# First batch of a spectral mixing and SwiGLU kernel: the first two chunks by turns, weights rounded in halves and loaded from ScalarE's queue

## The chip, the cores and the metric

One core of one Trainium2 chip. The metric is the device time in microseconds (us) of one execution. Each timed run is compared with runs of the kernel before on the same chip, in the same job.

## The reference

```python
X = np.fft.rfft(x, axis=1)                    # x: 8 x 3008 x 256
y = np.fft.irfft(X * (filt_r + 1j * filt_i)[None], n=3008, axis=1)
t = y.reshape(24064, 256)
g = t @ w_gate                                # 256 x 1536
out = (g / (1 + np.exp(-g)) * (t @ w_val)) @ w_out
```

## The kernel before

Each batch passes through a Fourier transform in two stages with tables, a filter, the inverse transform (stage 3 ends it) and the feed-forward part. That part works on four chunks of tokens; a chunk takes six blocks (`hidden`, one for each sixth of the 1536 columns) and, after every third of them, a projection (`project`). The products use a seven-product scheme for 2x2 blocks, so each of the 18 pieces of weight needs seven planes of 128 x 128 in memory: four from the weight, three sums. The next batch's transform fills in between.

The weights come as float64. They are turned to float32 by hand ("rounding"): VectorE takes mantissa and exponent apart, ScalarE converts, VectorE puts together, GpSimd multiplies both parts and makes the sums. This is done in the first 228 us, while the first batch runs. The parts that matter:

```python
def load_weights(j, queue=nc.sync):
    if j < len(weights):
        raws[j] = rpool.tile([128, 2, 2, 128, 2], U32, name=f"raw_{j}", tag="raw", bufs=2)
        for i in range(2):
            ins = queue.dma_start(out=raws[j][:, i], in_=weights[j][0][:, i])
            ...
def round_weights(j, following=True):
    if following:
        load_weights(j + 2)
    raw, (_, dst, left) = raws.pop(j), weights[j]
    low, high = raw[:, :, :, :, 0], raw[:, :, :, :, 1]
    pw = rpool.tile([128, 2, 2, 128], U32, name=f"pw_{j}", tag="pw")     # one buffer
    w = rpool.tile([128, 2, 2, 128], FP32, name=f"w_{j}", tag="w")       # one buffer
    ...  # VectorE: w <- high, pw <- high; ScalarE: w, pw; VectorE: pw, pw <- raw, w <- raw
    pin(e.tensor_tensor(out=dst[:, 0:4, :]..., in0=w, in1=pw.bitcast(FP32), op=ALU.mult))
    ...  # GpSimd: the four sums
for i in range(NP):                    # the blocks of a batch
    k, j = divmod(i, NJ)
    ...
    for _ in range((2, 3, 2, 2, 2, 3)[i] if todo else 0):
        round_weights(todo.pop(0))
    hidden(b, k, j, cur.y[k], fill)
```

A scheduler settles each engine's order when the kernel is built.

Of the kernel before, what the change touches and what calls it, by code (L numbers as in the profile page):

```python
# [34 lines left out]
FP32 = mybir.dt.float32  # L35
U32 = mybir.dt.uint32
AF = mybir.ActivationFunctionType
ALU = mybir.AluOpType
# [6 lines left out]
NJ = NM // 2  # L45
# [8 lines left out]
NCHUNK = 32 // NW  # L54
TH = NH * NR
TOK = (0, 128, TH - 128)
NQB = 2
JB = NJ // NQB
# [45 lines left out]
def kernel(  # L104
# [10 lines left out]
    nc = tc.nc  # L115
# [5 lines left out]
    def pool(name, bufs, space=None):  # L121
        kw = {} if space is None else {"space": space}
        return ctx.enter_context(tc.tile_pool(name=name, bufs=bufs, **kw))
# [19 lines left out]
    wv_t = cpool.tile([128, NJ, 7, 128], FP32)  # L143
# [17 lines left out]
    def add(eng, dst, a, b):  # L161
        eng.tensor_tensor(out=dst, in0=a, in1=b, op=ALU.add)  # L162

    def sub(eng, dst, a, b):
        eng.tensor_tensor(out=dst, in0=a, in1=b, op=ALU.subtract)  # L165
# [3 lines left out]
    def weight_parts():  # L169

        cols = [w.bitcast(U32).rearrange("(a p) (h j f two) -> j p h a f two",
                                         a=2, p=128, h=2, j=NJ, two=2)
                for w in (moe_w_gate, moe_w_val)]
        rows = moe_w_out.bitcast(U32).rearrange("(l j p) (c f two) -> j p l c f two",
                                                l=2, j=NJ, p=128, c=2, two=2)
        def hid(j):
            for w, dst in zip(cols, (wg_t, wv_t)):
                yield w[j], dst[:, j], True

        for q in range(NQB):  # L180
            for j in range(JB * q, JB * q + JB):
                yield from hid(j)
            for j in range(JB * q, JB * q + JB):
                yield rows[j], wo_t[:, j], False

    weights = list(weight_parts())
    raws = {}

    def load_weights(j, queue=nc.sync):
        if j < len(weights):  # L190
            raws[j] = rpool.tile([128, 2, 2, 128, 2], U32, name=f"raw_{j}", tag="raw", bufs=2)
            for i in range(2):
                ins = queue.dma_start(out=raws[j][:, i], in_=weights[j][0][:, i])
                if j in (2, 3):
                    tc.keep_in_program_order(ins)

    def round_weights(j, following=True):



        if following:
            load_weights(j + 2)
        raw, (_, dst, left) = raws.pop(j), weights[j]
        low, high = raw[:, :, :, :, 0], raw[:, :, :, :, 1]
        pw = rpool.tile([128, 2, 2, 128], U32, name=f"pw_{j}", tag="pw")
        w = rpool.tile([128, 2, 2, 128], FP32, name=f"w_{j}", tag="w")
        man = w.bitcast(U32)
        v = nc.vector
        flat = "p a b f -> p (a b f)"
        flat2 = "p a b f two -> p (a b f) two"  # L210

        pin = tc.keep_in_program_order
        pin(v.tensor_scalar(out=man, in0=high, scalar1=0xFFFFF, scalar2=None,
                            op0=ALU.bitwise_and))
        pin(nc.scalar.activation(out=w, in_=man, func=AF.Copy, scale=2.0 ** -20, bias=1.0))
        pin(v.tensor_scalar(out=pw, in0=high, scalar1=20, scalar2=0x7FF,
                            op0=ALU.logical_shift_right, op1=ALU.bitwise_and))
        pin(nc.scalar.activation(out=pw, in_=pw, func=AF.Relu, bias=off_t))
        v.tensor_scalar(out=pw, in0=pw, scalar1=255.0, scalar2=2.0 ** 23,
                        op0=ALU.min, op1=ALU.mult)  # L220
        v.scalar_tensor_tensor(out=pw.rearrange(flat), in0=raw.rearrange(flat2)[:, :, 1],
                               scalar=0x80000000, in1=pw.rearrange(flat),
                               op0=ALU.bitwise_and, op1=ALU.bitwise_or)
        v.scalar_tensor_tensor(out=w.rearrange(flat), in0=raw.rearrange(flat2)[:, :, 0],
                               scalar=2.0 ** -52, in1=w.rearrange(flat),
                               op0=ALU.mult, op1=ALU.add)

        e = nc.gpsimd
        pin(e.tensor_tensor(out=dst[:, 0:4, :].rearrange("p (a b) f -> p a b f", b=2), in0=w,  # L229
                            in1=pw.bitcast(FP32), op=ALU.mult))  # L230
        if left:
            a11, a12, a21, a22, s1, s2, s4 = [dst[:, i] for i in range(7)]
            add(e, s1, a21, a22)
            sub(e, s2, s1, a11)
            sub(e, a21, a11, a21)
            sub(e, s4, a12, s2)
        else:
            b11, b12, b21, b22, t1, t2, t4 = [dst[:, i] for i in range(7)]
            sub(e, t1, b12, b11)
            sub(e, t2, b22, t1)  # L240
            sub(e, b12, b22, b12)
            sub(e, t4, b21, t2)
# [3 lines left out]
    def bank(kind, name):  # L246
        return wps.tile([128, 512], FP32, name=f"w{kind}_{name}", tag=kind)

    def warm(count, width=4):


        for i in range(count):
            ps = bank("F", "idle")[:, 0:128 * width]
            tc.keep_in_program_order(nc.tensor.matmul(
                out=ps, lhsT=wv_t[:, 0, 0, :],
                rhs=wv_t[:, 0, 0:width, :].rearrange("p i f -> p (i f)"), start=True, stop=True))

    class Spectral:

# [277 lines left out]
    rpool = pool("raw", 1)  # L537
    todo = list(range(len(weights)))
# [7 lines left out]
    with tc.tile_pool(name="start", bufs=1) as spool0:  # L546
        for i in range(4):
            spec.load_x(i)
        spec.load_tables()
        load_weights(0, nc.scalar)  # L550
        load_weights(1, nc.scalar)
        nc.sync.dma_start(out=wi_t, in_=wi_dram.ap())
        nc.vector.memset(wv_t[:, 0], 0.0)
        warm(5)
        for u in range(N_ONE):
            spec.stage1(u)
            warm(1, 2)
        warm(6)
        for _ in range(2):
            round_weights(todo.pop(0), False)  # L560
        lag = 3
        for u in range(N_TWO + lag):
            if u < N_TWO:
                spec.stage2a(u)
            if u >= lag:
                spec.stage2b(u - lag)
    for j in (2, 3):
        load_weights(j)
    for i in range(2):
        spec.load_t4(0, i)  # L570
    warm(9)
# [2 lines left out]
    for _ in range(2):  # L574
        round_weights(todo.pop(0))
# [1 line left out]
    spool = pool("sp", 2)  # L577
    hpool = pool("hp", JB + 1)
    upool = pool("up", 2)
    opool = pool("op", 1)  # L580



# [2 lines left out]
    for b in range(B):  # L586
        cur = spec
        work = {}

        def at(i, piece):  # L590
            work.setdefault(i, []).append(piece)

        for k in range(1, NCHUNK):
            for i in range(2):
                at(NJ * (k - 1) + 1 + i, lambda k=k, i=i: cur.load_t4(k, i))
            for step in range(4):
                at(NJ * (k - 1) + 3 + step // 2, lambda k=k, step=step: cur.stage3(k, step))
        if b + 1 < B:
            spec = Spectral(b + 1)
            nxt = spec  # L600
            for u in range(N_ONE):
                at(u // 2, lambda u=u: nxt.stage1(u))
            for u in range(N_TWO + 1):
                if u:
                    at(9 + u, lambda u=u: nxt.stage2b(u - 1))
                if u < N_TWO:
                    at(9 + u, lambda u=u: nxt.stage2a(u))
            for i in range(2):
                at(22, lambda i=i: nxt.load_t4(0, i))
            for step in range(4):  # L610
                at(NP - 1, lambda step=step: nxt.stage3(0, step))

        for i in range(NP):
            k, j = divmod(i, NJ)
            pieces = work.get(i, [])
            first = (len(pieces) + 1) // 2
            fills = [pieces[:first], pieces[first:]]

            def fill(fills=fills):
                for piece in fills.pop(0):  # L620
                    piece()

            for _ in range((2, 3, 2, 2, 2, 3)[i] if todo else 0):
                round_weights(todo.pop(0))
            hidden(b, k, j, cur.y[k], fill)
            if late is not None:
                project(*late)
                late = None
            if j % JB == JB - 1:
                late = (b, k, j // JB)  # L630
# [31 lines left out]
```

## Time and profile before

| | before |
|---|---|
| time, median of 3 runs | 3118.65 us (3118.13 to 3119.42) |
| TensorE busy over the span | 98% |
| first product of stage 3 on TensorE | 103.0 us |
| last rounding instruction of VectorE starts | 222.5 us (ends 223.2) |

TensorE is the bound from 246 us on. All that can be won lies before. The prediction shows the lines.

To follow this I keep one ledger for every kernel. From the trace of TensorE I count its products up to a moment, one by one, give each the start-to-start distance that it has where TensorE is full (0.3157 us for 376 columns, 0.1117 for 128, 0.11 for 94, 0.43 for 512, 0.2155 for 256; warm-up products count nothing), and subtract the sum from the elapsed time. The rest is **lost time**. It needs no wait list, and sees slow clocks as well as gaps (in the kernel before, with a granted clock of 0.51 from 164 to 168 us, pairs of products of 376 columns took 1.34 to 1.62 us, later 0.80). Some records can be missing from a trace, so 1 or 2 us in it mean nothing.

### The profile page before, as it was taken

The numbers are of one execution on the slowest core, as the hardware profiler recorded it, in microseconds if no ns is written. First come the engines' busy times: TensorE is split into PE (matmuls) and PEld (weight loads), VectorE is DVE, ScalarE is ACT, GpSimd is POOL, SyncE is SP. The second block draws the span as 40 slices with busy tenths as digits, with TensorE's granted clock in tenths as the row PEclk, the third lists the DMA queues.
The fourth block names the chain that finished last, engine by engine and source line by source line (L and its number), as shares of the span: only waits on it lengthen the run. The fifth ranks groups of instructions, "written<-read, shape, count | busy, mean of one in ns | idle before, by whom it ended". The sixth has DMA issues, their size and how long they took to land.

```text
span 3116.7 us, 41163 instructions
## 1 busy us (share of the span) xinstructions
PE 3056.4 (98%) x15560; PEld 2240.5 (72%) x15560; DVE 1476.5 (47%) x2348; ACT 1140.3 (37%) x2070; POOL 1405.8 (45%) x1622
## 2 busy tenths in 40 slices
PE   7789999999999999999999999999999999999999
PEld 4457777777767777767777777767777677777776
DVE  4664553354543554345543455434553444544443
ACT  0443333333343343343333333343333433333333
POOL 3574454444543444444543454434544344533343
PEclk8999999999999999999999999999999999999999
DMA  8432222222212222222222132121322222200000
GB/s 233 130 117 68 72 81 56 61 76 68 75 55 72 59 79 60 61 68 81 69 60 65 57 88 71 51 71 55 91 68 56 63 63 68 68 28 21 21 6 16
DMA packets 123634, 212.51 MB, mean 68 GB/s; under 512 B 23670, under 2 KB 69750, under 8 KB 122578
## 3 DMA queue, kind: packets, MB, share of 16 engines
q1 hardware_dynamic: 91692, 132.25, 14.8%
q0 software_dynamic: 24448, 68.71, 7.7%
q10 hardware_dynamic: 7296, 8.92, 1.1%
q8 instruction: 123, 2.02, 0.3%
q14 instruction: 75, 0.61, 0.1%
HBM read 134.81 MB, written 74.97 MB: 67 GB/s over the span
## 4 chain that ended last, share of the span: by engine, by line
PE 80%; POOL 7%; DVE 6%; issue 3%; DMA 2%; ACT 2%; SPq 0%; POOLq 0%; ACTq 0%; DVEq 0%
PE wA_v L435 15%; PE wA_g L435 15%; PE wA_o L499 7%; PE wE_v L435 7%; PE wE_g L435 7%; PE wE_o L499 7%; PE wF_o L499 4%; PE wF_g L435 4%; PE pd L396 3%; PE wF_v L435 3%; POOL o L162 3%; PE pa L332 3%; POOL h L165 3%; PE pc L376 2%; PE pb L356 2%
## 5 line engine op out<-in xcount | busy, mean ns | idle before, releaser
L435 PE MATMUL wA_v<-y,wv_t 128*128 128x376 f32 x1536 | 612.5, 480 | 7.3 <-ACT u_v L444 4.3
L435 PE MATMUL wA_g<-y,wg_t 128*128 128x376 f32 x1536 | 614.3, 481 | 4.4 <-POOL wg_t L229 3.5
L165 POOL TENSOR_TENSOR h<-h 128x376 f32<-128x376 f32 x576 | 566.9, 984 | 28.8
L162 POOL TENSOR_TENSOR h<-h 128x376 f32<-128x376 f32 x192 | 188.4, 981 | 701.2 <-PE wE_v L435 389.1
L444 ACT COPY u_g<-wA_g 128x376 f32<-128x376 f32 x576 | 269.5, 468 | 589.9 <-PE wA_g L435 587.6
L435 PEld LDWEIGHTS wA_v<-y,wv_t 128*128 128x128 f32 x1536 | 289.2, 190 | 204.0 <-DVE h L457 15.6
L499 PEld LDWEIGHTS wA_o<-wo_t,h 128*128 128x128 f32 x3456 | 406.3, 192 | 16.3
L499 PE MATMUL wA_o<-wo_t,h 128*128 128x128 f32 x3456 | 417.5, 275 | 0.0
L435 PEld LDWEIGHTS wA_g<-y,wg_t 128*128 128x128 f32 x1536 | 281.1, 190 | 172.3 <-issue 28.1
L462 ACT ACTIVATE s<-s 128x1128 f32<-128x1128 f32 x192 | 219.5, 1143 | 373.2 <-DVE s L162 373.2
L464 DVE TENSOR_TENSOR h<-s,h 128x1128 f32<-128x1128 f32 x192 | 257.1, 1339 | 124.0 <-ACT s L462 124.0
L435 PE MATMUL wE_g<-y,wg_t 128*128 128x376 f32 x768 | 307.1, 482 | 2.1 <-DVE s L162 2.1
L435 PE MATMUL wE_v<-y,wv_t 128*128 128x376 f32 x768 | 306.1, 480 | 1.8 <-DVE h L162 1.6
L444 ACT COPY u_v<-wA_v 128x376 f32<-128x376 f32 x576 | 272.2, 473 | 69.3 <-PE wA_v L435 65.2
L162 DVE TENSOR_TENSOR s<-u_g,wE_g 128x376 f32<-128x376 f32 x384 | 208.9, 544 | 176.2 <-ACT u_g L444 174.6
L162 DVE TENSOR_TENSOR s<-u_g,wF_g 128x376 f32<-128x376 f32 x192 | 104.4, 544 | 394.9 <-PE wF_g L435 369.3
L499 PE MATMUL wE_o<-wo_t,h 128*128 128x128 f32 x2304 | 281.6, 276 | 7.5 <-DVE o L162 7.5
L499 PE MATMUL wF_o<-wo_t,h 128*128 128x128 f32 x2304 | 278.5, 275 | 0.0
L499 PEld LDWEIGHTS wE_o<-wo_t,h 128*128 128x128 f32 x2304 | 267.4, 192 | 13.6 <-DVE o L162 13.6
L499 PEld LDWEIGHTS wF_o<-wo_t,h 128*128 128x128 f32 x2304 | 267.8, 192 | 0.3
L162 POOL TENSOR_TENSOR p<-p,q 128x512 f32<-128x512 f32 x96 | 121.6, 1266 | 226.4 <-DVE q L367 226.4
L162 DVE TENSOR_TENSOR h<-u_v,wE_v 128x376 f32<-128x376 f32 x384 | 208.9, 544 | 26.5 <-ACT u_v L444 5.1
(86 smaller groups left out, 3275.3 us busy)
## 6 DMA issues: line engine op xcount, KB each, us to landing
t<-d SPq DMA_DIRECT2D x192, 128.0 KB
t<-d SPq DMA_DIRECT2D x64, 384.0 KB
d<-t POOLq DMA_DIRECT2D x112, 192.0 KB, 2.5
tb<-de_tbl SPq DMA_DIRECT2D x84, 256.0 KB
d<-g POOLq DMA_DIRECT2D x168, 128.0 KB, 2.8
x<-in_x_dram SPq DMA_DIRECT2D x112, 160.0 KB
out_dram<-o POOLq DMA_DIRECT2D x128, 128.0 KB, 2.0
f<-in_filt_r_dram SPq DMA_DIRECT2D x168, 64.0 KB
```

The lines of the kernel that those rows point to most:

```text
L162: eng.tensor_tensor(out=dst, in0=a, in1=b, op=ALU.add)
L165: eng.tensor_tensor(out=dst, in0=a, in1=b, op=ALU.subtract)
L332: nc.tensor.matmul(out=ps[0:NK], lhsT=wf_t, rhs=self.x.pop(u), start=True, stop=True)
L356: nc.tensor.matmul(out=ps[:, i, :], lhsT=self.tb[u][:, i, 0, :], rhs=t2[:, i, :], start=True, stop=True)
L376: nc.tensor.matmul(out=ps[:, i, :], lhsT=tb[:, i, 1, :], rhs=pt[:, i, :], start=True, stop=True)
L396: nc.tensor.matmul(out=psv[:, n, :], lhsT=self.t4[k, i][:, n, ts(cb, 128)], rhs=wi_t, start=True, stop=True)
L435: nc.tensor.matmul(out=bk[z][kind], lhsT=wt[z][:, j, LEFT[p], :], rhs=y[:, RIGHT[p], :], start=start, stop=True, skip_group_check=True)
L444: nc.scalar.copy(out=u[(1, 6, 7).index(p)], in_=bk[z]["A"])
L462: nc.scalar.activation(out=s[:, 0:3], in_=s[:, 0:3], func=AF.Silu)
L464: nc.vector.tensor_tensor(out=h[:, 0:3], in0=s[:, 0:3], in1=h[:, 0:3], op=ALU.mult)
L499: nc.tensor.matmul(out=bk[kind][:, t, :], lhsT=hs[i][:, HID[p], t0:t0 + 128], rhs=wo_t[:, JB * q + i, WO[p], :], start=start and t == 0 an ...
```

## The change

The intent: let the first chunk's first three blocks be followed by the second chunk's first three, which use the same weights, so that rounding has more time; make the turns of rounding shorter by halves; free SyncE's queue of weight loads, which stood 66.9 us and kept inputs behind it.

```diff
-            raws[j] = rpool.tile([128, 2, 2, 128, 2], U32, name=f"raw_{j}", tag="raw", bufs=2)
+            raws[i] = p.tile([128, 2, 128, 2], U32, name=f"raw_{i}", tag="raw", bufs=2)
...
-    def round_weights(j, following=True):
-        if following:
-            load_weights(j + 2)
-        pw = rpool.tile([128, 2, 2, 128], U32, name=f"pw_{j}", tag="pw")
-        w = rpool.tile([128, 2, 2, 128], FP32, name=f"w_{j}", tag="w")
+    def round_half(i):
+        pw = rpool.tile([128, 2, 128], U32, name=f"pw_{i}", tag="pw")
+        w = rpool.tile([128, 2, 128], FP32, name=f"w_{i}", tag="w")
...
         pin(nc.scalar.activation(out=pw, in_=pw, func=AF.Relu, bias=off_t))
+        if i + 1 >= START:
+            load_weights(i + 1, nc.scalar, True)
...
-        nc.vector.memset(wv_t[:, 0], 0.0)
-        warm(5)
         for u in range(N_ONE):
             spec.stage1(u)
-            warm(1, 2)
-        warm(6)
...
-    opool = pool("op", 1)
+    opool = pool("op", 2)
...
+        order = [(k, q) for k in range(NCHUNK) for q in range(NQB)]
+        if b == 0:
+            order[1:3] = order[2:0:-1]
+        steps = [(k, JB * q + i) for k, q in order for i in range(JB)]
...
-            for _ in range((2, 3, 2, 2, 2, 3)[i] if todo else 0):
+            for _ in range((2, 1, 1, 2, 2, 2, 1, 1, 1, 1)[i] if todo else 0):
```

Cut: views for the halves, the initial loads, the places of stage 3 for the second chunk. The halves have a second purpose: two chunks under way need two output buffers, and by the tile sizes in the two kernels the halves free just what the second one takes, 6 KB a partition (the two buffers of raw shrink from 8 KB to 4, pw and w from 2 to 1 each).

More of the change, by code (lines that the diff above doesn't have):

```diff
@@ L187, with load_weights @@
     raws = {}
-    def load_weights(j, queue=nc.sync):
-        if j < len(weights):
-            raws[j] = rpool.tile([128, 2, 2, 128, 2], U32, name=f"raw_{j}", tag="raw", bufs=2)
-            for i in range(2):
-                ins = queue.dma_start(out=raws[j][:, i], in_=weights[j][0][:, i])
-                if j in (2, 3):
-                    tc.keep_in_program_order(ins)
-    def round_weights(j, following=True):
-        if following:
-            load_weights(j + 2)
-        raw, (_, dst, left) = raws.pop(j), weights[j]
-        low, high = raw[:, :, :, :, 0], raw[:, :, :, :, 1]
-        pw = rpool.tile([128, 2, 2, 128], U32, name=f"pw_{j}", tag="pw")
-        w = rpool.tile([128, 2, 2, 128], FP32, name=f"w_{j}", tag="w")
+    START = 6
+    def load_weights(i, queue=nc.sync, hold=False):
+        if i < 2 * len(weights):
+            p = spool0 if 2 <= i < 4 else rpool
+            raws[i] = p.tile([128, 2, 128, 2], U32, name=f"raw_{i}", tag="raw", bufs=2)
+            ins = queue.dma_start(out=raws[i], in_=weights[i // 2][0][:, i % 2])
+            if hold:
+                tc.keep_in_program_order(ins)
+    def round_half(i):
+        raw, dst = raws.pop(i), weights[i // 2][1]
+        low, high = raw[:, :, :, 0], raw[:, :, :, 1]
+        pw = rpool.tile([128, 2, 128], U32, name=f"pw_{i}", tag="pw")
+        w = rpool.tile([128, 2, 128], FP32, name=f"w_{i}", tag="w")
         man = w.bitcast(U32)
         v = nc.vector
-        flat = "p a b f -> p (a b f)"
-        flat2 = "p a b f two -> p (a b f) two"
+        flat = "p b f -> p (b f)"
+        flat2 = "p b f two -> p (b f) two"
         pin = tc.keep_in_program_order
@@ L226, in round_weights @@
                                op0=ALU.mult, op1=ALU.add)
+        pin(nc.gpsimd.tensor_tensor(out=dst[:, ts(i % 2, 2), :], in0=w, in1=pw.bitcast(FP32),
+                                    op=ALU.mult))
+    def round_weights(j):
+        for i in (2 * j, 2 * j + 1):
+            round_half(i)
+        _, dst, left = weights[j]
         e = nc.gpsimd
-        pin(e.tensor_tensor(out=dst[:, 0:4, :].rearrange("p (a b) f -> p a b f", b=2), in0=w,
-                            in1=pw.bitcast(FP32), op=ALU.mult))
         if left:
@@ L247, in bank, with warm @@
         return wps.tile([128, 512], FP32, name=f"w{kind}_{name}", tag=kind)
-    def warm(count, width=4):
+    def warm(count):
         for i in range(count):
-            ps = bank("F", "idle")[:, 0:128 * width]
+            ps = bank("F", "idle")
             tc.keep_in_program_order(nc.tensor.matmul(
                 out=ps, lhsT=wv_t[:, 0, 0, :],
-                rhs=wv_t[:, 0, 0:width, :].rearrange("p i f -> p (i f)"), start=True, stop=True))
+                rhs=wv_t[:, 0, 0:4, :].rearrange("p i f -> p (i f)"), start=True, stop=True))
     class Spectral:
@@ L549 @@
         spec.load_tables()
-        load_weights(0, nc.scalar)
-        load_weights(1, nc.scalar)
+        for i in range(4):
+            load_weights(i, nc.scalar)
         nc.sync.dma_start(out=wi_t, in_=wi_dram.ap())
-        nc.vector.memset(wv_t[:, 0], 0.0)
-        warm(5)
         for u in range(N_ONE):
             spec.stage1(u)
-            warm(1, 2)
-        warm(6)
         for _ in range(2):
-            round_weights(todo.pop(0), False)
+            round_weights(todo.pop(0))
         lag = 3
@@ L566 @@
                 spec.stage2b(u - lag)
-    for j in (2, 3):
-        load_weights(j)
+    for i in range(4, 6):
+        load_weights(i, hold=True)
     for i in range(2):
@@ L591, in at @@
             work.setdefault(i, []).append(piece)
+        order = [(k, q) for k in range(NCHUNK) for q in range(NQB)]
+        if b == 0:
+            order[1:3] = order[2:0:-1]
+        steps = [(k, JB * q + i) for k, q in order for i in range(JB)]
         for k in range(1, NCHUNK):
+            start = steps.index((k, 0))
             for i in range(2):
-                at(NJ * (k - 1) + 1 + i, lambda k=k, i=i: cur.load_t4(k, i))
+                at(max(start - 5 + i, 0), lambda k=k, i=i: cur.load_t4(k, i))
             for step in range(4):
-                at(NJ * (k - 1) + 3 + step // 2, lambda k=k, step=step: cur.stage3(k, step))
+                at(start - 3 + step // 2 if start > 3 else 1 + step // 2,
+                   lambda k=k, step=step: cur.stage3(k, step))
         if b + 1 < B:
@@ L613 @@
         for i in range(NP):
-            k, j = divmod(i, NJ)
+            k, j = steps[i]
             pieces = work.get(i, [])
```

## The prediction

> **What bounds the kernel now.** I read the page first, for where TensorE is not full, then a table of stretches, the timelines of TensorE and VectorE from 100 to 250 us, and the waits, of the DMA queues too. From the page, busy tenths and granted clock in 40 slices of 78 us:
>
> ```profile
> PE   7789999999999999999999999999999999999999
> ...
> PEclk8999999999999999999999999999999999999999
> ```
>
> Only the first three slices are not full. By stretch (TensorE, weight load, VectorE, ScalarE, GpSimd busy; clock; DMA):
>
> ```profile
> 0.00:103.00 103.00, 78.64 (x201) 42.70 (x202) 50.52 (x76) 10.87 (x17) 30.68 (x42) 0.85 0.78 212
> 103.00:165.00 62.00, 44.70 (x149) 22.68 (x148) 44.49 (x68) 31.19 (x53) 46.18 (x52) 0.94 0.40 125
> 165.00:192.00 27.00, 25.61 (x157) 20.38 (x156) 15.12 (x26) 9.98 (x19) 17.57 (x22) 0.95 0.29 88
> 192.00:246.00 54.00, 50.94 (x241) 34.61 (x240) 34.90 (x56) 24.04 (x45) 38.66 (x46) 0.97 0.34 104
> ...
> 1000.00:2000.00 1000.00, 997.45 (x5140) 739.55 (x5139) 477.46 (x761) 373.50 (x680) 452.34 (x519) 1.00 0.24 68
> ```
>
> From about 246 us on TensorE is the bound, and the change leaves its work there alone. All there is to win lies before. The stretch to 103 us is the first batch's transform: DMA share 0.78, then VectorE's p and q products back to back (55 to 91 us). From 103 us feed-forward blocks run while the weights are still being rounded, and there TensorE waits:
>
> ```profile
> 151.67 1.93 PE L332 MATMUL pa<-x,wf_t 94*96 94x512 f32 x4 [2.83 <-DMA x<-in_x_dram]
> 153.43 2.17 PE L396 MATMUL pd<-wi_t,t 96*128 96x94 f32 x16
> 158.63 2.02 PE L332 MATMUL pa<-x,wf_t 94*96 94x512 f32 x2 [3.02 <-ACT y L407]
> 164.16 1.62 PE L435 MATMUL wA_g<-y,wg_t 128*128 128x376 f32 x2 [3.50 <-POOL wg_t L229]
> ```
>
> Rounding is a chain, since its tiles w and pw have one buffer: VectorE starts the next weight only when GpSimd's product has read them. One turn of it on VectorE, with the block's additions in between:
>
> ```profile
> 119.86 0.43 DVE L213 TENSOR_SCALAR w<-raw 128x512 uint32<-128x512 uint32 x1 [0.54 <-POOL wv_t L229]
> 120.21 0.69 DVE L216 TENSOR_SCALAR pw<-raw 128x512 uint32<-128x512 uint32 x1
> 120.81 0.55 DVE L162 TENSOR_TENSOR s<-u_g,wE_g 128x376 f32<-128x376 f32 x1
> 121.27 0.93 DVE L224 SCALAR_TENSOR_TENSOR w<-raw,w 128x512 f32<-128x512 uint32 x1
> ...
> 126.26 0.43 DVE L213 TENSOR_SCALAR w<-raw 128x512 uint32<-128x512 uint32 x1 [1.16 <-POOL wg_t L229]
> ```
>
> Turns start at 114.5, 119.9, 126.3 and 134.6 us: 5.4 to 8.3 us each. SyncE's queue stands still behind the next weight's load, which waits for a raw buffer, and the inputs of the next batch stand behind it:
>
> ```profile
> SPq L193 <- DVE pw L221: 66.9, 13, 15.0
> ```
>
> **How much there is to win.** In the full part the start-to-start distances are 0.63 us for a product of a block (14 a block: 8.84), 14.07 for one projection, 0.88 for a step of stage 3 and 0.86 for a stage-1 tile. From 102.99 to 245.09 us the timeline holds 7 blocks (61.9), 2 projections (28.1), 8 stage-3 steps (7.0) and 14 stage-1 tiles (12.0): 109.0 us of work in 142.1. So 33 us, 1.06% of the run, is the most that the stretch can give. By 191.77 us, the end of the first projection, 28 of them are lost; 5 come after.
>
> [...]the tensor_scalar on raw (L216) takes 0.42 at best, 0.68 as the median, 1.22 at most. [...]after the wait at 164.16 a product pair takes 1.62 us where others take 0.80.
>
> **The change, part by part.**
>
> *Warm-up matmuls at the start* go (5 ahead of stage 1, 16 within it, 6 after it; the 9 before stage 3 stay). Stage 1 is paced by its writes: the chain of waits holds 10.5, 7.5 and 6.2 us of them. A cold stage-1 tile takes 1.7 us, while the copies come on average every 2.2 us (16 between 10 and 45 us), and at 22 to 27 and 40 to 60 us the clock is cold now too, with the warm-ups in the way. I put -0.5 to +2, say +1 us.
>
> *Halves.* [...]the trace's whole is 3.36 (sum of the five medians 0.43, 0.68, 0.88, 0.68, 0.69)[...].
>
> *Loads.* All but six halves are now issued by ScalarE inside the half before: one ahead, where before it was a whole weight or two. Its latency is exposed: first tensor_scalar 0.3, two ScalarE passes 0.45 each, issue 0.4, landing. The landings known are 2.0 us for 128 KB and 2.5 for 192 KB, which extends to 3.0 for 256 KB:
>
> ```profile
> d<-t POOLq DMA_DIRECT2D x112, 192.0 KB, 2.5
> ...
> out_dram<-o POOLq DMA_DIRECT2D x128, 128.0 KB, 2.0
> ```
>
> Sum 4.6 us a half, 9.2 a weight, more than the present 5.4 to 8.3. SyncE's queue, though, is free for inputs, so the waits on x (2.8 us) go.
>
> *Order.* The second chunk's first three blocks come before the first chunk's last three. So ten instead of six blocks run until the last weight is needed, and no new weight matters between the third block and the seventh, except the three of the first projection.
>
> *The sum.* [...]TensorE's work to the same point: 10 x 8.84 + 28.1 + 7.0 + 13.8 = 137 us, to 240. [...]By the chain of loads: halves 4 and 5 are there, half 4 starts at 109, half 6 at 116.6, half 7 at 121, then one per 4.6 us: weight 3 is ready at 124 (now 120), weight 5 at 142.5 (now 134.6). The third block ends near 150, as now (148), but with more stage-1 and stage-3 work behind it. The fourth block then needs nothing new (now it waits to 164) and ends near 161. The first projection needs weight 8, half 17, at 170, and with its block ends near 183. Work to there: 4 x 8.84 + 14.1 + 7.0 + 6.0 = 62.5 and one or two tiles more, from 103 to 165.5. Lost: 17.5 us. After it the halves (last near 252) stay just ahead of their blocks. So of 33 us some 18 remain: **3118.65 - 33 + 18 + 1 = 3105 us**.
>
> **Rivals.** (1) *The load's latency is what VectorE waits for, all along*: it takes instructions in order, so every missed half holds up block additions behind it. 30 halves, each 1 us late, cost 30 us and eat the gain: 3118 to 3122. For it: the one-ahead load[...]. Against: the scheduler puts 1.9 us of block work between halves, which covers part of a landing. (2) *Reordering pays nearly whole*: landings are nearer 2 us, halves follow each other every 3.6 us, the projection's weights are ready at 155. Then 8 us remain lost: 3095. For it: the DMA share in the stretch is only 0.3 to 0.6. Against: stage-1 writes and inputs share the engines just then. (3) [...]Against: stage 2's first products are cold now as well (1.94 us a group at 55 us).
>
> **Range and chances.** The middle is my chain; rival 2 sets the lower edge with some us beyond, 3092; rival 1 in half measure and rival 3 the upper, 3116. Two per cent would be 62 us; the stretch has 33 to give, and no rival costs more than about 10. Faster 0.005, same 0.985, slower 0.01.
>
> **What would show it.** In the changed profile: no SyncE wait for weight loads; first block products near 104 us (past 106: the warm-ups mattered); VectorE or ScalarE waits of 1 to 3 us on raw's DMA in most halves (none: rival 2); first projection done near 183 us; no TensorE gap in the fourth block; work without gaps from about 190. Wrong would be gaps still there at 190 to 250 us (rival 1), or a changed rhythm after 260 us, of which I expect nothing.

Of VectorE's sum until the last half, which came to 126 us from 107.7, to 234, the term for the halves had no trace behind it; with it the whole sum is cut, and what was drawn from it: that there was hardly any slack, and that halves cost VectorE somewhat more and TensorE nothing. Its measured part, 10 blocks of 5.14 us (7 additions or products of 0.54, one of 1.34) and 8 us for stage 3 and the projections, makes 1.9 us of block work for each of 32 halves. "The same point" in TensorE's sum is the last half. Rival 3: that the missing warm-ups would slow the products into stage 2. "Cold" stands for a low granted clock: 0.50 from 22 to 27 us, 0.74 from 40 to 60 and 0.66 from 54 to 59 in the kernel before. The terms of "sum 4.6 us a half" are my estimates. The changed kernel shows 0.28 us at the shortest for the first tensor_scalar, 0.42 and 0.50 on average for ScalarE's passes and 0.33 to 0.43 for an issue; a load of 256 KB took 2.6 to 4.4 us to land, median 3.0 (e_free_after). Where the prediction and the expectations say that an engine takes its instructions in order, the traces show the case told with the kernel before (135.57 us).

## More of the kernel before

In the kernel before, VectorE stood idle for 2.24 us up to 134.63, until GpSimd's product was done, and a block's addition whose product on TensorE had ended at 131.5 us started at 135.57, behind two instructions of rounding; TensorE waited 0.61 us for it.

## The result, and the profile after

The changed kernel takes 3121.09 us (median of 4 runs, 3119.53 to 3122.58), beside 3118.39 (3117.44 to 3119.42) for the kernel before in the same job. The ratio is 1.0009, 95% interval 0.9991 to 1.0026: no difference. A ratio here and below is the mean time of one kernel's fast runs over that of the other's of the same rounds, so not quite the ratio of the medians quoted. The prediction was 3105, with 3092 to 3116.

From the page, 40 slices of 78 us (busy tenths of TensorE):

```profile
PE   6889999999999999999999999999999999999999
```

The second slice is a little fuller than before (8 where it was 7) and the first emptier (6 where it was 7), as the warm-ups that are gone had counted as busy; from the third on nothing differs. The table of stretches, changed kernel, one line cut (TensorE, weight load, VectorE, ScalarE, GpSimd busy; clock; DMA share; GB/s):

```profile
103.00:165.00 62.00, 52.89 (x189) 30.28 (x188) 41.13 (x85) 32.58 (x64) 32.47 (x45) 0.97 0.49 136
165.00:192.00 27.00, 20.80 (x137) 17.82 (x136) 19.25 (x34) 9.19 (x19) 16.41 (x24) 0.94 0.23 64
...
246.00:300.00 54.00, 51.28 (x263) 37.02 (x262) 34.55 (x66) 22.58 (x45) 33.51 (x43) 1.00 0.21 59
```

The gain is there, and it is given back. TensorE is busy 8.2 us more up to 165 us, 4.8 less from there to 192, and 2.7 less from 246 to 300, where it was full before (54.00 of 54). The ledger says the same:

| lost time (us) up to | 106 | 150 | 165 | 190 | 246 | 300 |
|---|---|---|---|---|---|---|
| before | 69.6 | 82.1 | 92.1 | 95.6 | 101.5 | 101.4 |
| changed | 71.2 | 81.9 | 84.7 | 92.9 | 98.2 | 102.6 |

At 165 us the changed kernel is 7.4 us ahead; at 190 only 2.7 us of this are left, and at 300 it is 1.2 us behind. The timeline of TensorE in the changed kernel, where it stood over a microsecond between 145 and 200 us:

```profile
150.36 1.30 PE L442 MATMUL wE_v<-y,wv_t 128*128 128x376 f32 x2 [3.11 <-POOL wv_t L162]
...
169.54 0.49 PE L506 MATMUL wF_o<-wo_t,h 128*128 128x128 f32 x2 [3.22 <-POOL wo_t L229]
181.88 3.24 PE L506 MATMUL wA_o<-wo_t,h 128*128 128x128 f32 x14 [2.98 <-POOL wo_t L165]
```

The third block waits for its last weight, the fourth runs without a gap, and the first projection waits twice for weights. That projection ends at 192.7 us. The first instructions of the halves on VectorE stand 5.15 us apart on average (111.9 to 271.7 us, 31 steps), so a weight takes 10.3 us where it took 7.3 before (109.2 to 219.2 us, 15 steps), and VectorE's part of rounding ends at 274.2 us instead of 223.2. SyncE's queue no longer stands behind a buffer of the weights (66.9 us of waiting for VectorE's reading of raw before, no such wait in its list now), as intended.

What rounding costs VectorE: all groups of it between 103 and 300 us (busy us, mean ns of one | idle just before). Kernel before, 16 weights:

```profile
L224 DVE SCALAR_TENSOR_TENSOR w<-raw,w 128x512 f32<-128x512 uint32 x16 | 13.9, 869 | 0.8 <-ACT w L215 0.5
L221 DVE SCALAR_TENSOR_TENSOR pw<-raw,pw 128x512 uint32<-128x512 uint32 x16 | 13.6, 848 | 0.2
L216 DVE TENSOR_SCALAR pw<-raw 128x512 uint32<-128x512 uint32 x16 | 11.7, 731 | 0.0
L219 DVE TENSOR_SCALAR pw<-pw 128x512 uint32<-128x512 uint32 x16 | 11.6, 724 | 0.2 <-ACT pw L218 0.2
...
L213 DVE TENSOR_SCALAR w<-raw 128x512 uint32<-128x512 uint32 x16 | 7.4, 461 | 16.9 <-POOL wg_t L229 8.8 <-POOL wo_t L229 5.3 <-POOL wv_t L229 2.8
```

Changed kernel, 32 halves:

```profile
L226 DVE SCALAR_TENSOR_TENSOR w<-raw,w 128x256 f32<-128x256 uint32 x32 | 19.4, 607 | 3.6 <-ACT w L214 3.5
L223 DVE SCALAR_TENSOR_TENSOR pw<-raw,pw 128x256 uint32<-128x256 uint32 x32 | 18.8, 589 | 0.7
...
L221 DVE TENSOR_SCALAR pw<-pw 128x256 uint32<-128x256 uint32 x32 | 15.1, 471 | 0.1
L212 DVE TENSOR_SCALAR w<-raw 128x256 uint32<-128x256 uint32 x32 | 14.2, 445 | 17.7 <-POOL wo_t L229 6.7 <-DMA raw<-in_moe_w_val_dram 3.5 <-POOL wg_t L229 3.3
...
L215 DVE TENSOR_SCALAR pw<-raw 128x256 uint32<-128x256 uint32 x32 | 13.0, 406 | 0.0
```

The first sums to 58.2 us, 3.64 a weight; the second to 80.5, 5.03 a weight. An instruction of half the elements takes 56 to 97% of the time of a whole one, not 50. At their shortest, halves and wholes take 0.28 and 0.42 us for tensor_scalar, 0.41 and 0.68 for scalar_tensor_tensor. On pw, without raw's step of two words, tensor_scalar takes 0.27 and 0.41. But the shortest times give only 0.28 x 3 + 0.41 x 2 = 1.66 us for a half. Measured are 2.52: scalar_tensor_tensor to w, for one, takes 607 ns on average where 410 is the shortest (whole ones 869 and 679). What makes it longer no run separates.

### The profile page after: what moved, and what is told of

Read it like the earlier page. It is cut to its first block, busy times and chain, and to the rows that moved or that the text cites. A ratio compares the mean times of both kernels' runs of the same rounds, so it can differ in the third digit from the quotient of the medians.

```text
span 3117.8 us, 41190 instructions
## 1 busy us (share of the span) xinstructions
PE 3047.1 (98%) x15506; PEld 2231.0 (72%) x15506; DVE 1495.3 (48%) x2437; ACT 1146.6 (37%) x2106; POOL 1399.4 (45%) x1640
## 4 chain that ended last, share of the span: by engine, by line
PE 78%; POOL 8%; DVE 6%; issue 3%; DMA 2%; ACT 2%; SPq 0%; POOLq 0%; DVEq 0%; ACTq 0%
PE wA_v L442 15%; PE wA_g L442 15%; PE wE_g L442 7%; PE wE_v L442 7%; PE wA_o L506 7%; PE wE_o L506 7%; PE wF_o L506 4%; PE wF_g L442 4%; PE pd L403 3%; PE wF_v L442 3%; POOL o L162 3%; POOL h L165 3%; PE pa L339 3%; PE pc L383 2%; PE pb L363 2%
```

## The experiments

| run | what it is | ratio to before | 95% interval |
|---|---|---|---|
| e_warm | changed + warm-ups | 1.0009 | 0.9996 to 1.0023 |
| e_before_nowarm | before - warm-ups | 1.0003 | 0.9991 to 1.0016 |
| e_w2 | changed, two buffers of w and pw | 0.9989 | 0.9977 to 1.0002 |
| e_raw3 | changed, ScalarE's loads two ahead | 1.0033 | 1.0020 to 1.0045 |
| e_free_before | before, rounding's passes out | 0.9923 | 0.9911 to 0.9936 |
| e_free_after | changed, the same | 0.9990 | 0.9976 to 1.0003 |
| e_halves_oldorder | halves and ScalarE's loads, old order | 1.0116 | 1.0102 to 1.0130 |
| e_pace | changed, rounding placed earlier | 1.0005 | 0.9992 to 1.0019 |
| e_sync2 | changed, SyncE's loads | 1.0016 | 1.0003 to 1.0028 |
| e_sync3 | the same, three raw buffers | 1.0032 | 1.0019 to 1.0044 |
| e_old_sync4 | halves, old order, before's loads | 1.0064 | 1.0052 to 1.0077 |
| e_whole_act | before, ScalarE's loads | 0.9999 | 0.9986 to 1.0013 |
| e_order_whole_ip | new order, whole weights | **0.9948** | 0.9934 to 0.9962 |
| e_old_ip | before, w and pw in place | 0.9991 | 0.9979 to 1.0004 |
| e_order_whole_ip_act | new order, whole, ScalarE's loads | 0.9946 | 0.9933 to 0.9958 |
| e_halves_ip | new order, halves, in place | 0.9989 | 0.9977 to 1.0002 |
| e_order_whole_ip_pace | new order, whole, evener places | 0.9948 | 0.9934 to 0.9962 |

0.1% is 3.1 us. All runs but the two e_free were correct.

### The start: warm-ups

e_warm puts the removed `warm(...)` calls back into the changed kernel; e_before_nowarm takes them out of the one before.

> The changed kernel with the removed warm-up matmuls of the start put back; nothing else differs. Theory A (the missing warm-ups alone delay the start): the first stage-3 product, at 105.7 us in the changed kernel and 103.0 in the one before, comes back to 103.0 to 103.5, and the time falls by 2 to 3 us, to about 3118.5. Rival (the two extra turns of rounding in the start, or the order of the weight loads, delay it): first stage-3 product stays at 105 or later, time unchanged.

> The kernel before without those warm-ups, else unchanged. Theory A: first stage-3 product at 105 to 106 us, time up by 2 to 3 us to about 3121. Rival: 103.0 us, time unchanged.

Measured: 3124.03 us (3119.47 to 3125.45) and 3120.74 (3118.99 to 3122.27). The first product of stage 3 comes at 103.0 (before) and 106.4 us (e_warm) with warm-ups, at 105.7 (changed), 105.5, 103.6 and 103.8 (e_before_nowarm, e_w2, e_raw3) without. It varies by 3 us from run to run whatever the warm-ups are. They cost and win nothing that these runs can show.

### The single buffers, and the landing of the loads

```diff
 # e_w2
-        pw = rpool.tile([128, 2, 128], U32, name=f"pw_{i}", tag="pw")
-        w = rpool.tile([128, 2, 128], FP32, name=f"w_{i}", tag="w")
+        pw = rpool.tile([128, 2, 128], U32, name=f"pw_{i}", tag="pw", bufs=2)
+        w = rpool.tile([128, 2, 128], FP32, name=f"w_{i}", tag="w", bufs=2)
 # e_raw3
-            raws[i] = p.tile(..., tag="raw", bufs=2)
+            raws[i] = p.tile(..., tag="raw", bufs=2 if 2 <= i < 4 else 3)
-        if i + 1 >= START:
-            load_weights(i + 1, nc.scalar, True)
+        if i + 2 >= START + 1:
+            load_weights(i + 2, nc.scalar, True)
```

> The changed kernel with two buffers each for the tiles w and pw. Theory G (in the feed-forward stretch the rounding product stands in GpSimd's queue behind a block's additions, and VectorE, with one buffer, stands behind the product): VectorE's waits for GpSimd before the first rounding instruction (about 14 us) go, a half every 4.3 us instead of 5.2, last half near 250 instead of 274 us, TensorE's lost time between 106 and 300 us falls from 31 to about 22, time down 6 to 10 us. Rival L (the landing of the load that is issued only one half ahead is the limit): the waits move to the load, time within 2 us of the changed kernel.

> The changed kernel with three raw buffers and loads issued two halves ahead. Rival L: VectorE's waits for raw loads go, a half every 4.3 us, time down 6 to 10 us. Theory G: those waits (5.5 us in all) go, others on GpSimd take their place, time down 0 to 3 us.

Measured: 3118.61 us (3112.29 to 3119.06) and 3130.25 (3127.75 to 3132.15). Two buffers win perhaps 6 us against the changed kernel (0.9989 against 1.0009, intervals that overlap). But theory G's sign is missing: the last half starts at 271.2 us, not near 250 (changed: 271.7). Loads two ahead end every wait of VectorE for a raw buffer's data, and the kernel is 10 us slower than before, not faster. In the timeline of VectorE the halves now come in bunches 2.8 to 3.7 us apart with holes of 13 and 17 us, and the last half starts at 280.2 us (changed: 271.7). The landing is not what sets the end.

### Rounding without its passes

In both kernels the five VectorE and two ScalarE passes go; GpSimd multiplies raw words instead.

```diff
-        pin(v.tensor_scalar(out=man, in0=high, ...))
-        ...                                # all passes of VectorE and ScalarE
+        hi = high.bitcast(FP32)
-        pin(e.tensor_tensor(out=dst[...], in0=w, in1=pw.bitcast(FP32), op=ALU.mult))
+        pin(e.tensor_tensor(out=dst[...], in0=hi, in1=hi, op=ALU.mult))
```

> Kernel before with the rounding's five VectorE and two ScalarE passes taken out (result wrong on purpose); loads, GpSimd's product and its sums stay. Theory R, rounding's passes on the in-order VectorE and ScalarE are what TensorE loses its 33 us by: the loss between the first feed-forward product and 300 us falls below 12 us, and the time to about 3097 (3093 to 3103). Rival D, the loads and GpSimd's product and sums hold TensorE up: the time falls by less than 8 us, to 3110 or more.

> Changed kernel with the same passes taken out (result wrong on purpose). Theory R: about 3097 (3093 to 3103), within 4 us of the kernel before so treated, since the new order has then nothing to win. Rival L, the one-ahead load from ScalarE's queue is what holds the changed kernel: it stays at 3110 or more, and at least 8 us above the kernel before so treated, as each load is then still waited for.

Measured: 3095.51 us (3092.89 to 3100.13) and 3116.35 (3114.74 to 3118.47). For the kernel before, theory R holds: without the passes it loses 8.3 us from 106 to 300 us (69.6 to 77.9 in the ledger) instead of 31.8. The passes on VectorE and ScalarE are 24 of the 33 us. The changed kernel did what rival L said, and I took this for the loads. That was a misreading, and the experiment is confounded: with the passes gone, a raw buffer is freed by GpSimd's product, and ScalarE's load issue waits for it in ScalarE's own order, with the block's copies behind: before copies of u_g ScalarE sat idle until such a product was done 4 times, 14.5 us in all. From 100 to 310 us of e_free_after TensorE's products wait 8 times, 13.3 us in all, for ScalarE's copy of u_g. Such waits are new here (the list of the kernel before so treated has none by a product). In the changed kernel the list has no wait of ScalarE for GpSimd, and each issue takes 0.33 to 0.43 us (in e_free_after up to 1.60).

### The old order with halves, and the places of rounding

```diff
 # e_halves_oldorder, against the changed kernel
-    opool = pool("op", 2)
+    opool = pool("op", 1)
-            k, j = steps[i]
+            k, j = divmod(i, NJ)
-            for _ in range((2, 1, 1, 2, 2, 2, 1, 1, 1, 1)[i] if todo else 0):
+            for _ in range((2, 3, 2, 2, 2, 3)[i] if todo else 0):
 # e_pace, against the changed kernel
+            for _ in range((2, 2, 2, 2, 2, 2, 2, 0, 0, 0)[i] if todo else 0):
```

> Changed kernel with the old order of blocks and the old places of the rounding (2,3,2,2,2,3 weights a block), one output buffer; halves and ScalarE's loads stay. Theory O, the order wins some 8 us in the fourth block and the halves with their loads cost as much: 3126 to 3132, ratio to before 1.002 to 1.005, with the wait before the fourth block longer than before's. Rival N, the order gains nothing and the halves cost nothing: 3117 to 3122.

> Changed kernel with two weights placed ahead of each of the first seven blocks in place of 2,1,1,2,2,2,1,1,1,1, so that the last weight of the first projection is placed ahead of the third block, not the fourth. Theory P, the place in the program makes that weight late: the first projection ends near 187 us, not 192.7, rounding ends before 255, time 3113 to 3117. Rival G, the engines' queues set the pace of the halves (5.1 us each) wherever they are placed: the first projection ends within 2 us of 192.7 and the time is 3119 to 3124.

Measured: 3155.89 us (3154.82 to 3156.81) and 3121.50 (3117.67 to 3124.88). The first is far beyond what either theory said. With halves and ScalarE's loads the old order costs 36 us more than the kernel before, and the new order takes some 33 of them back (1.0116 to 1.0009). So the order does win, and something else in the change costs as much. One stretch of e_halves_oldorder shows how, in the columns used above:

```profile
165.00:192.00 27.00, 20.91 (x36) 8.24 (x35) 12.43 (x31) 9.92 (x21) 11.87 (x20) 0.50 0.73 227
```

36 product instructions where the kernel before has 157, and a granted clock of 0.50: the timeline shows stage-1 and stage-3 tiles for most of 20 us and no block, as the weights are late. The places in the program (e_pace) do not change the time, and the first projection ends at 192.6 us (changed: 192.7): in this rival G held. They do move the end of rounding, from 274.2 to 263.6 us, so it is too much to say that the halves follow their queues alone.

### Loads or halves

```diff
 # e_sync2 (changed kernel, loads from SyncE; e_sync3: i + 3, three raw buffers)
     def round_half(i):
+        if i + 2 >= 6:
+            load_weights(i + 2)
-        if i + 1 >= START:
-            load_weights(i + 1, nc.scalar, True)
 # e_old_sync4: the same in e_halves_oldorder, i + 4, four raw buffers
 # e_whole_act (kernel before, loads from ScalarE)
-        if following:
-            load_weights(j + 2)
         pin(nc.scalar.activation(out=pw, in_=pw, func=AF.Relu, bias=off_t))
+        if j + 1 >= 4:
+            load_weights(j + 1, nc.scalar)
```

> Changed kernel, the loads of the halves issued from SyncE's queue again, the second next half at the top of each half (it starts when the buffer of the half just read is free); buffers, halves and order stay. Theory L (the load one ahead in ScalarE's order costs the time): halves start 4.0 to 4.5 us apart, rounding ends before 255 us, time 3108 to 3114. Theory H (halves as such, each a round trip VectorE-ScalarE-VectorE-GpSimd in queues served in order, set about 5 us whatever the load does): 3118 to 3124, rounding ends after 265.

> As the run with SyncE's loads, with a third buffer, so loads up to three halves ahead. Theory L: as good or up to 3 us better, 3106 to 3114. Theory H: no better than the changed kernel, 3118 to 3130 (the run with three buffers and ScalarE's loads took 3130).

> Kernel of halves in the old order, with four half buffers loaded from SyncE's queue: the loads of the kernel before, its order, its places of rounding; only the halves (and the missing warm-ups) are new. Theory L: back to 3118 to 3126. Theory H: stays near the 3156 of the run with ScalarE's loads, 3145 to 3158.

> Kernel before (whole weights, old order, warm-ups), with the next weight's load issued by ScalarE after its second pass, one weight ahead, in place of SyncE two ahead: only the loads are new. Theory L: 3140 or more, since a whole weight's landing is waited for. Theory H: 3117 to 3126.

Measured: 3122.81 us (3122.32 to 3125.80), 3129.41 (3124.47 to 3132.28), 3139.17 (3136.70 to 3141.08), 3118.76 (3114.45 to 3120.33). Theory L falls three times: ScalarE's one-ahead loads cost the kernel before nothing, and taking them out of the changed kernel wins nothing. Theory H stands, with one correction: in the old order halves cost some 20 us with the loads of before and 36 with one-ahead loads, so there the depth of the loads is worth some 16 us, probably since that order needs each weight as soon as it can be had.

### The order alone, and the halves alone

For the missing cell, whole weights in the new order, w and pw need no buffers of their own: w is put where the weight will lie, pw into the planes of its sums and the first plane of the next weight.

```diff
 # e_order_whole_ip: order, places and output buffers of the changed kernel,
 # rounding and loads of the kernel before, and
-    wg_t = cpool.tile([128, NJ, 7, 128], FP32)               # wv_t, wo_t alike
+    wg_p = cpool.tile([128, NJ * 7 + 1, 128], FP32, name="wg_t")
+    wg_t = wg_p[:, 0:NJ * 7].rearrange("p (j i) f -> p j i f", i=7)
-        pw = rpool.tile([128, 2, 2, 128], U32, name=f"pw_{j}", tag="pw")
-        w = rpool.tile([128, 2, 2, 128], FP32, name=f"w_{j}", tag="w")
+        w = room[:, 0:4].rearrange("p (a b) f -> p a b f", b=2)   # room: planes 7 j to 7 j + 7
+        pw = room[:, 4:8].rearrange("p (a b) f -> p a b f", b=2).bitcast(U32)
 # e_old_ip: kernel before with these lines; e_order_whole_ip_act: loads as in e_whole_act
 # e_halves_ip: e_order_whole_ip with the passes and the product in two halves
+        for h in range(2):
+            r, w = raw[:, h], room[:, 2 * h:2 * h + 2]
+            pw = room[:, 4 + 2 * h:6 + 2 * h].bitcast(U32)
             ...
 # e_order_whole_ip_pace
-            for _ in range((2, 1, 1, 2, 2, 2, 1, 1, 1, 1)[i] if todo else 0):
+            for _ in range((2, 1, 1, 1, 2, 1, 2, 1, 2, 1)[i] if todo else 0):
```

> The new order and places of rounding with whole weights and SyncE's loads two ahead. To make room for the second output buffer, w and pw lie in the weight's own planes (pw runs into the first plane of the next). Theory H (the halves cost what the order wins): 3098 to 3110, rounding ends before 235 us. Rival O (the order wins only against a program that is late for another reason, and nothing against whole weights): 3115 to 3122.

> Kernel before with w and pw in the weight's own planes, as in the run above, nothing else: what these places alone are worth. If the single buffers of w and pw hold the kernel before up (8 of its turns follow GpSimd's product by about a microsecond): 3108 to 3115. If not: 3117 to 3121.

> As the first run, but loads from ScalarE's queue, one weight ahead: with whole weights the loads should be of no weight in the new order either (theory H: within 4 us of the first run). Rival L2 (one-ahead loads cost more in the new order, which asks for weights more evenly): 5 us or more above it.

> The 3103-us kernel (new order, whole weights, w and pw in the weight's planes, SyncE's loads two weights ahead) with the passes and the product done in two halves; loads, buffers, order and places stay, no half waits for the other's product. Theory H (twice as many turns through three engines' queues cost the time): 3114 to 3122, and VectorE is busier by 7 to 12 us between 103 and 300 us. Rival B (it was the single buffers and the shallow loads of the changed kernel, not the halves): 3102 to 3107.

> The 3103-us kernel with the rounding placed more evenly (2,1,1,1,2,1,2,1,2,1 weights ahead of the blocks). What is left there is 15 us between 103 and 300 us, 6 of it by 155 us and 3 around 157 to 160 us. If the places make it: 3098 to 3102. If it is the work on VectorE as such: 3102 to 3107.

Measured: 3103.33 us (3101.82 to 3106.64), 3117.70 (3114.97 to 3119.37), 3103.89 (3100.41 to 3105.47), 3113.79 (3112.40 to 3116.95), 3100.67 (3099.51 to 3105.62). The new order with whole weights is correct, beats both kernels, and lands where my prediction put the change as a whole. "New order" here takes in what came with it: the places of rounding, the second output buffer and the missing warm-ups. The places of w and pw alone do not do it, ScalarE's loads cost it nothing, and evener places of rounding win nothing (the same ratio). My expectation that rounding would end before 235 us there was wrong: VectorE's part ends at 254.9, at no cost.

The same kernel with halves loses 0.41% of it again, 12.8 us (13.1 beside e_order_whole_ip_pace, which ran in the same job). Its loads, buffers, order and places are those of the 3103-us kernel, so this is the price of the halves as such. I had expected 3114 to 3122; the single buffers and shallow loads of the changed kernel are then the rest. The wait lists of TensorE from 103 to 300 us (their largest groups; total, times, longest) show what became of the waits. Changed kernel:

```profile
PE wE_v L442 <- POOL wv_t L162: 4.3, 2, 3.1
PE wF_o L506 <- POOL wo_t L229: 3.2, 1, 3.2
PE wA_v L442 <- ACT u_v L451: 3.1, 3, 1.3
PE wA_o L506 <- POOL wo_t L165: 3.0, 1, 3.0
```

New order with whole weights:

```profile
PE wA_g L437 <- ACT u_g L446: 3.3, 3, 1.5
PE wE_g L437 <- DVE s L165: 3.1, 3, 1.5
PE wE_v L437 <- DVE h L165: 1.9, 2, 1.4
```

The halves in place:

```profile
PE wE_g L435 <- DVE s L165: 3.7, 3, 1.9
PE wA_v L435 <- ACT u_v L444: 3.6, 5, 1.3
PE wA_g L435 <- ACT u_g L444: 3.5, 5, 1.4
```

In the changed kernel TensorE waits 10.5 us for weights (`wv_t`, `wo_t`). In the other two it waits for no weight, only for the blocks' own copies and additions on ScalarE and VectorE, more often with halves. Ledger, lost time up to 106, 165 and 300 us: whole 68.2, 78.7, 84.5; halves 68.9, 82.5, 95.4. Rounding's groups on VectorE in this stretch, added up as above, are 70.0 us with whole weights and 89.5 with halves: 19.5 us more in VectorE's order. The two profiled executions are 10.6 us apart (3101.82 and 3112.40), and the ledger accounts for it: 16.3 us lost from 106 to 300 us with whole weights, 26.5 with halves. Some 6 us of the difference are distances between products that are less than half a us too long, some 4 are longer ones. VectorE's busy time as a whole rose by 4.6 us only (140.8 to 145.4), less than the 7 to 12 I expected; it ran 114 instructions other than rounding's in the stretch where it had run 126.

VectorE is not the only engine whose order the halves fill. Rounding's passes on ScalarE go from 32 to 64, 21.6 to 29.4 us. And of TensorE's waits in the full lists those for ScalarE grow more, from 5.3 to 9.1 us, those for VectorE from 6.3 to 7.3. One of them in the kernel with halves in place, all engines (lines between them cut):

```profile
250.53 0.42 ACT L217 ACTIVATE wo_t<-wo_t 128x256 f32<-128x256 uint32 x1 [1.14 <-DVE wo_t L215]
...
250.85 0.45 ACT L444 COPY u_v<-wA_v 128x376 f32<-128x376 f32 x1
...
251.45 0.87 PE L435 MATMUL wA_v<-y,wv_t 128*128 128x376 f32 x2 [1.00 <-ACT u_v L444]
```

The product that u_v copies had ended at 249.2 us. Its copy stood behind a half's pass on ScalarE, and that pass waited for VectorE's pass of the same half, which took 1.07 us (at the shortest 0.28). So the delay is handed on from VectorE through ScalarE. No run gives the halves to one engine alone, so how much each order adds is not shown. More work on VectorE by itself need not cost anything: in e_old_ip rounding's groups on VectorE add up to 65.3 us, 7 more than before, and the time is the same.

## Why the prediction was wrong

In per cent of the time before: in place alone -0.09, the new order -0.43 (0.9991 to 0.9948), halves +0.41 (to 0.9989), the rest of the change +0.20 (to 1.0009). In us: -2.8, -13.4, +12.8, +6.2; together +2.8. Each term has an interval of some 5 us to both sides, by the widths above. The order and the halves are shown. The last 6 us are as large as what e_w2 wins back with two buffers, so probably the single buffers of w and pw; the runs do not prove it.

- **What bounds it, and 33 us as the most: right.** Taking rounding's passes out wins 24 us of it.
- **Warm-ups, "say +1 us": no effect shown.** The first block products came at 107.7 us, past the 106 that was to be the sign of missing warm-ups; with the warm-ups back (e_warm) they came at 108.3.
- **Halves, expected to cost VectorE somewhat more and TensorE nothing: this step failed.** A weight in halves takes 5.03 us of VectorE against 3.64, 22.3 us more for 16 weights; I had expected less, by terms that no trace showed. The greater error is "TensorE nothing". VectorE and ScalarE have time to spare as an average (busy 135.8 and 91.2 of the 197 us from 103 to 300 in the changed kernel), but a block's copy or addition waits behind a half in its engine's order, and TensorE waits for it (1.00 us at 251.45 in e_halves_ip). With nothing else changed, halves put 19.5 us more into VectorE's order and 7.8 into ScalarE's, and 12.8 us appear in the time. I had counted VectorE alone and overlooked the way through ScalarE.
- **Loads, "its latency is exposed ... 4.6 us a half": the number came near (5.15), the reason was wrong.** Where VectorE waited for a landing, the half started 2.9 to 4.0 us after its issue (once 5.5), as predicted. But it waited so before 8 of 32 halves only, 5.5 us in all, not before most of them. And with loads ahead (e_raw3, e_sync2, e_sync3) the last half started at 280.2, 273.4 and 280.5 us, not before the changed kernel's 271.7. A chain that I left out is GpSimd's: its product for a half stands in its own order behind block additions, and the next half waits for it, as w and pw have one buffer. In the changed kernel's timeline GpSimd adds an h at 163.6 us, makes the product at 164.6, and VectorE starts the next half at 165.3, after 1.6 us of idling. But this chain alone does not set the pace either: with two buffers (e_w2) the last half started at 271.2 us. With neither chain, in e_halves_ip, it still started at 260.5; what sets the pace of the halves stays open.
- **Order: right in mechanism.** The fourth block ran without a gap, as I said. The first projection ended at 192.7 us, not 183, after waits for weights. With whole weights it runs from 162 to 177, but with halves in place from 167 to 181, so the halves as such are not what made it so late; the single buffers and shallow loads are left, not told apart.
- **The sum, "of 33 us some 18 remain": wrong for the change, right for the order without halves.** That kernel loses 16 us from 106 to 300 us, and takes 3103 us.
- **"After it the halves stay just ahead of their blocks": wrong.** From 190 us to 300 nearly 10 us more are lost, 4 of them after 246 us, where rounding still ran and I expected nothing.
- **Rival 1** gave the right time (3118 to 3122) for the wrong cause, which is luck, and I took it at half measure only. Late halves do hold up block work, but making the landing earlier did not cure it, and the halves' own instructions cost 12.8 us without any wait of TensorE for a weight.

## What to carry to other kernels

Splitting a chain of passes into halves did not halve its turns here: a tensor_scalar of 256 elements took 0.28 us at the shortest where one of 512 took 0.42, and what was added stood in front of other work on VectorE and ScalarE. Before calling extra work on a half-idle engine free, ask what stands behind it in its order and who waits for that, and ask it of every engine that the chain passes through. When a change has several parts and moves nothing, build the parts singly; here one part was worth 13 us and another cost 13, and a memory limit that had tied them together could be got round by putting scratch data where the result would lie.
